# Float64 weights made into float32: the lower word as a rounded integer and one integer add on GpSimd

## The chip, the core and the metric

The kernel runs on one core of a Trainium2 chip. Time is device microseconds from the start to the end of one execution. Five engines run their own instruction streams: TensorE (PE, matrix products; PEld is its loading of weights), VectorE (DVE), ScalarE (ACT), GpSimd (POOL) and SyncE (SP, which here issues all DMAs). They wait for each other by semaphores.

## What is computed

Attention with pooled keys and values, and then two feed-forward layers over 4608 tokens, 512 features and 2048 hidden units:

```python
k_p, v_p = mean of k, v over 8 neighbours along the sequence
x = softmax(q @ k_p.T / sqrt(64)) @ v_p          # 8 batches, 8 heads, 576 tokens, head size 64
h = x @ moe_w_in;  g = maximum(0.01 * h, h);  x = g @ moe_w_out
h = x @ moe2_w_in
g = where(h >= 1, h, where(h <= -1, 0, (h + 1) ** 2 / 4))
out = (g @ moe2_w_out).astype(float32)
```

The four weight matrices (512x2048 and 2048x512) come in as float64. The kernel takes them in as pairs of 32-bit words and makes float32 values of the bits.

## The kernel before

Tokens are worked on in blocks of 512. Each float32 matrix is held as a high and a low part, of which three products are summed, so that every product of 128x128 by 512 columns costs three matmuls (lines 598 to 600 for the first matrix of a layer, "h", and 625 to 627 for the second, "acc").

The program is written in program order by hand: generators yield after each group of instructions, and `run` and `pump` go round them, so the text order of the yields sets what stands next to what on each engine. There are nine blocks. The first visit is block 0 with the hidden units 0 to 1023 (f = 0 to 7), the second block 1 with all 2048 (f = 0 to 15), the third block 0 again with f = 8 to 15, and then the other blocks one after another. Each visit has two slots for one f. In the first visit and before it, the attention of blocks 0 and 1 is computed beside the first weights; the weights of the first layer arrive one tile of 128x512 at a time (26 whole tiles and 12 half tiles, of 6 tiles more), until the end of the second visit. In later visits the second layer's weights are converted in halves of 128x256 (64 of them) and stored to DRAM as float32.

One weight tile is converted by `to_f32` out of `bits`, in which the low and the high word of each float64 alternate (`lo`, `hi`: each a strided view, with a step of two words). Names in the rows: `wb` is the tile of bits, `wc` the result, whose left half is `a` (the float32 value) and whose right half is `e` (the exponent), `w0i` and `w0o` the high and low parts of layer 0's two matrices. Line 108 (ScalarE) takes the absolute value of the high word read as float32, line 109 (VectorE) clamps it, line 111 (ScalarE) turns the low word into a float scaled by 2^-52, line 112 (VectorE) shifts the exponent into place, line 116 (VectorE) joins sign, exponent and the upper 20 bits of the fraction into `a`, line 120 (VectorE) masks out the power of two of `a`, line 122 (GpSimd) multiplies it with the scaled low word, and line 123 (GpSimd) adds the product to `a`. Then line 133 (ScalarE) copies `a` rounded to the high part, and line 135 (VectorE) takes the difference for the low part. Line 135 is also that of other splits (`gl`, `aL`, `aX`); in the first visit the split of `gl` is on GpSimd.

GpSimd's other work in the first visits is the normalisation of the attention weights (line 455), which follows VectorE's sums (lines 444 to 452).

Of the kernel before, what the change touches and what calls it, by code (L numbers as in the profile page):

```python
# [8 lines left out]
F32 = mybir.dt.float32  # L9
F32R = mybir.dt.float32r  # L10
U32 = mybir.dt.uint32
AF = mybir.ActivationFunctionType
ALU = mybir.AluOpType
# [22 lines left out]
def attention_moe_moe2(ctx: ExitStack, tc: tile.TileContext, qT, kT, v, k01, v01, w_in1, w_out1, w_in2, w_out2, out):  # L36
# [5 lines left out]
    nc = tc.nc  # L42
# [40 lines left out]
    def bits_load(key, part, n, tile_of):  # L83

        layer, kind, f = key
        t = tile_of([P, 2 * DM // n], U32, f"wb{layer}{kind}{f}_{part}")
        w_in, w_out = w_bits[layer]
        if kind == "i":
            kn = KT // n
            src = w_in[part * kn * P:(part + 1) * kn * P, 2 * f * P:2 * (f + 1) * P]  # L90
            nc.sync.dma_start(
                out=t.rearrange("p (k c) -> p k c", k=kn), in_=src.rearrange("(k p) c -> p k c", p=P)
            )
        else:
            nc.sync.dma_start(out=t, in_=w_out[f * P:(f + 1) * P, 2 * DM // n * part:2 * DM // n * (part + 1)])
        w_raw[key, part] = t

    def to_f32(key, part, n, tile_of):


        layer, kind, f = key
        bits = w_raw.pop((key, part)).rearrange("p (n t) -> p t n", t=2)
        lo, hi = bits[:, 0], bits[:, 1]
        c = tile_of([P, 2 * DM // n], U32, f"wc{layer}{kind}{f}_{part}")
        a, e = c[:, 0:DM // n], c[:, DM // n:]
        ef, lof = e.bitcast(F32), lo.bitcast(F32)
        w_f32[key, part] = a.bitcast(F32)
        nc.scalar.activation(out=ef, in_=hi.bitcast(F32), func=AF.Abs)
        nc.vector.tensor_scalar(out=ef, in0=ef, scalar1=LEAST, scalar2=MOST, op0=ALU.max, op1=ALU.min)
        yield True  # L110
        nc.scalar.activation(out=lof, in_=lo, func=AF.Copy, scale=2.0**-52)
        nc.vector.tensor_scalar(
            out=e, in0=e, scalar1=5, scalar2=2, op0=ALU.logical_shift_left, op1=ALU.logical_shift_right
        )
        yield True
        nc.vector.scalar_tensor_tensor(
            out=a, in0=hi, scalar=0xC0000000, in1=e, op0=ALU.bitwise_and, op1=ALU.bitwise_or
        )
        yield True
        nc.vector.tensor_scalar(out=e, in0=a, scalar1=0xFF800000, scalar2=None, op0=ALU.bitwise_and)  # L120
        yield True
        nc.gpsimd.tensor_tensor(out=ef, in0=lof, in1=ef, op=ALU.mult)
        nc.gpsimd.tensor_tensor(out=a.bitcast(F32), in0=a.bitcast(F32), in1=ef, op=ALU.add)

    def w_tiles(key):
        layer, kind, f = key
# [11 lines left out]
    def f32_keep(key, part, n):  # L138
        hi, lo = w_tiles(key)
        return split(hi[:, cols(part, n)], lo[:, cols(part, n)], w_f32.pop((key, part)))  # L140
# [1025 lines left out]
    with tc.manual_schedule():  # L1166
# [3 lines left out]
            out=mask, in_=ident[0:96, 0:96].rearrange("p (g c i) -> p c g i", g=3, c=4), axis=AX.XY, op=ALU.add  # L1170
# [28 lines left out]
        def first_weights(key, part, n, raw_of, f32_of):  # L1199

            bits_load(key, part, n, raw_of)
            yield True
            yield True
            turn = to_f32(key, part, n, f32_of)
            for step in (1, 3, 1, 0):
                for _ in range(step):
                    next(turn, None)
                yield True
            yield from f32_keep(key, part, n)
# [3 lines left out]
        def later_weights():  # L1213

            i = state["late"]
            state["late"] += 1
            gens = []
            if 0 <= i - 2 < len(rest_jobs):
                key, part, n, _, tile_of = rest_jobs[i - 2]
                gens.append(to_f32(key, part, n, tile_of))  # L1220
            if 0 <= i - 4 < len(rest_jobs):
                gens.append(f32_keep(*rest_jobs[i - 4][:3]))
            if i < len(rest_jobs):
                loads.append((bits_load, *rest_jobs[i][:4]))
            return gens
# [8 lines left out]
        def weights_up_to(n):  # L1234
            for job in jobs[state["step"]:n]:
                active.append(first_weights(*job))
            state["step"] = max(state["step"], min(n, len(jobs)))
# [79 lines left out]
        def second_weights(load):  # L1317
            def turn(h):
                yield from to_f32(*h, f32_tile)
                f32_store(*h)  # L1320

            gens = [turn(h) for h in pending2]
            n = state["step2"]
            state["step2"] += 1
            pending2[:] = halves2[len(halves2) * n // n_steps2:len(halves2) * (n + 1) // n_steps2] if load else []
            for h in pending2:
                loads.append((bits_load, *h, raw_tile))
            return gens
# [91 lines left out]
```

## Time and profile before

| | |
|---|---|
| median of 3 runs | 1757.46 us (1756.05 to 1760.45) |
| span of the profiled execution, first to last instruction | 1755.2 us |
| TensorE busy | 1674.8 us, 95% of the span |
| VectorE busy | 1204.4 us, 69% |
| ScalarE busy | 868.3 us, 49% |
| GpSimd busy | 662.7 us, 38% |
[...]

The profiled execution has no time of its own beside its span, so the span is held against the median of the runs; the two differ by 2.3 us, which covers what lies around the first and the last instruction and the difference from run to run. Busy shares are means over stages: to see what one stage waits for, it is read by itself, with the busy time of each engine in it and with the chain of work that ended last. [...] "Idle before" is time in which an engine had nothing running, and what ended it.

### The profile page before, as it was taken

Reading aid. Unit: us, or ns where it says so; the run is one execution under the profiler, and the core shown is the slowest. Engines: PE = TensorE matmul, PEld = TensorE weight load, DVE = VectorE, ACT = ScalarE, POOL = GpSimd, SP = SyncE. Lnnn points to the kernel's source line nnn. Section 1 sums busy time; section 2 is a strip of 40 time slices with the busy share of each in tenths; the row PEclk is TensorE's granted clock in tenths of the full one; section 3 lists DMA queues with packets and bytes.
Section 4 is the critical chain, followed back from the end, with each engine's and each line's share of the span. In section 5 each row is a group of like instructions: output and inputs, shape, how many; then the busy total and the mean of one; then the engine's idle time right before and its main releaser. Section 6 shows DMA issues by size and latency. Waiting matters only on the chain.

```text
span 1755.2 us, 27818 instructions
## 1 busy us (share of the span) xinstructions
PE 1674.8 (95%) x9372; PEld 1477.4 (84%) x9372; DVE 1204.4 (69%) x2294; ACT 868.3 (49%) x1873; POOL 662.7 (38%) x750
## 2 busy tenths in 40 slices
PE   6778999999999999999999999999999799999998
PEld 4566778778888888888888898899899799999998
DVE  7987864565655555564435577877866788887967
ACT  4545443434444343443334566776666444544444
POOL 4664521222222222221224345454443525242525
PEclk9889999999999999999999999999999999999999
DMA  6423332323232231322222264564435873444231
GB/s 211 138 83 96 121 123 78 99 68 112 69 102 82 69 109 55 115 75 72 58 94 57 77 227 170 182 237 168 172 135 206 313 253 123 137 150 140 103 109 61
DMA packets 154223, 221.51 MB, mean 126 GB/s; under 512 B 18592, under 2 KB 95392, under 8 KB 154080
## 3 DMA queue, kind: packets, MB, share of 16 engines
q1 hardware_dynamic: 154080, 219.73, 38.6%
q8 instruction: 74, 1.21, 0.3%
q14 instruction: 69, 0.57, 0.1%
HBM read 136.84 MB, written 82.84 MB: 125 GB/s over the span
## 4 chain that ended last, share of the span: by engine, by line
PE 70%; DVE 15%; DMA 6%; issue 4%; ACT 3%; POOL 1%; SPq 0%; DVEq 0%; ACTq 0%; POOLq 0%
PE u L1083 20%; PE acc L625 6%; PE acc L626 6%; PE acc L627 6%; PE h L598 6%; PE h L599 6%; PE h L600 6%; PE Y L841 4%; PE V L841 2%; PE X L841 2%; PE sc L422 2%; PE tm L478 1%; DMA g<-tV 1%; DVE xs L702 1%; DVE tW L893 1%
## 5 line engine op out<-in xcount | busy, mean ns | idle before, releaser
L1083 PE MATMUL u<-v,m 128*128 128x256 f32 x3024 | 366.9, 284 | 8.0 <-DVE m L1048 8.0
L1083 PEld LDWEIGHTS u<-v,m 128*128 128x128 f32 x3024 | 364.8, 192 | 10.1 <-DVE m L1048 9.7
L1048 DVE TENSOR_TENSOR m<-m,m 128x512 fp32r<-128x512 f32 (+1 forms) x280 | 249.7, 922 | 55.2 <-ACT m L1043 47.6
L1043 ACT ACTIVATE m<-m 128x512 fp32r<-128x512 f32 (+1 forms) x280 | 162.8, 588 | 190.8 <-PE u L1083 134.5
L626 PE MATMUL acc<-gl,w0o 128*128 128x512 f32 x576 | 228.2, 396 | 10.2 <-DVE gl L135 10.2
L625 PE MATMUL acc<-gh,w0o 128*128 128x512 f32 x576 | 233.0, 405 | 1.3 <-ACT gh L133 1.2
L599 PE MATMUL h<-xl,w0i 128*128 128x512 f32 x576 | 226.6, 393 | 6.4 <-DVE xl L184 5.6
L598 PE MATMUL h<-xh,w0i 128*128 128x512 f32 x576 | 230.4, 400 | 0.3 <-DMA xh<-xk 0.3
L135 DVE TENSOR_TENSOR gl<-t,gh 128x512 fp32r<-128x512 f32 x136 | 102.0, 750 | 185.5 <-ACT gh L133 179.9
L627 PE MATMUL acc<-gh,w0o 128*128 128x512 f32 x576 | 226.8, 394 | 0.0
L600 PE MATMUL h<-xh,w0i 128*128 128x512 f32 x576 | 226.2, 393 | 0.0
L609 ACT ACTIVATE t<-h 128x512 f32<-128x512 f32 x144 | 85.9, 597 | 188.3 <-PE h L600 110.3
L455 POOL TENSOR_TENSOR at<-at,r 128x32 f32<-128x32 f32 (+3 forms) x160 | 75.3, 491 | 198.7 <-DVE r L452 185.9
L626 PEld LDWEIGHTS acc<-gl,w0o 128*128 128x128 f32 x576 | 109.4, 190 | 34.0 <-DVE gl L135 13.5
L599 PEld LDWEIGHTS h<-xl,w0i 128*128 128x128 f32 x576 | 109.1, 189 | 29.6 <-DVE xl L184 6.7
L625 PEld LDWEIGHTS acc<-gh,w0o 128*128 128x128 f32 x576 | 109.2, 190 | 27.1 <-ACT gh L133 3.1
L598 PEld LDWEIGHTS h<-xh,w0i 128*128 128x128 f32 x576 | 109.3, 190 | 23.9 <-DMA xh<-xk 1.1
L627 PEld LDWEIGHTS acc<-gh,w0o 128*128 128x128 f32 x576 | 109.3, 190 | 23.3
L600 PEld LDWEIGHTS h<-xh,w0i 128*128 128x128 f32 x576 | 109.0, 189 | 22.9
L882 POOL TENSOR_SCALAR tV<-tV 128x384 f32<-128x384 f32 x48 | 58.4, 1216 | 151.4 <-ACT tV L874 126.0
L841 PE MATMUL Y<-xs,v 128*128 128x384 f32 x432 | 87.1, 338 | 8.7 <-DVE p L860 8.1
L133 ACT ACTIVATE gh<-t 128x512 fp32r<-128x512 f32 x144 | 91.0, 632 | 4.5
(280 smaller groups left out, 3199.9 us busy)
## 6 DMA issues: line engine op xcount, KB each, us to landing
m<-g SPq DMA_DIRECT2D x128, 256.0 KB
w2d<-w2o SPq DMA_DIRECT2D x56, 256.0 KB
v<-w2d SPq DMA_DIRECT2D x28, 512.0 KB
x<-o SPq DMA_DIRECT2D x36, 256.0 KB
xr<-x SPq DMA_DIRECT2D x24, 384.0 KB
g<-tX SPq DMA_DIRECT2D x48, 192.0 KB
g<-tV SPq DMA_DIRECT2D x48, 192.0 KB
g<-tW SPq DMA_DIRECT2D x48, 192.0 KB
```

The lines of the kernel that those rows point to most:

```text
L133: nc.scalar.activation(out=hi, in_=src, func=AF.Copy)
L135: engine.tensor_tensor(out=lo, in0=src, in1=hi, op=ALU.subtract)
L598: nc.tensor.matmul(ph, wh[:, c], xh, start=k == 0, stop=False)
L599: nc.tensor.matmul(ph, wh[:, c], xl, start=False, stop=False)
L600: nc.tensor.matmul(ph, wl[:, c], xh, start=False, stop=k == KT - 1)
L625: nc.tensor.matmul(acc, wh[:, c], gh, start=st, stop=False)
L626: nc.tensor.matmul(acc, wh[:, c], gl, start=False, stop=False)
L627: nc.tensor.matmul(acc, wl[:, c], gh, start=False, stop=sp)
L841: nc.tensor.matmul(ps, w[:, c], x[k, i], start=begin and k == n == 0, stop=k == 1 and n == 2, skip_group_check=True,)
L1043: nc.scalar.activation(out=self.s[u][0], in_=self.unit_source(u), func=AF.Copy)
L1048: nc.vector.tensor_tensor(out=lo, in0=self.unit_source(u), in1=hi, op=ALU.subtract)
L1083: nc.tensor.matmul(ps, a[:, c], w, start=begin and i == 0, stop=f == self.NJ - 1 and i == 2, skip_group_check=True,)
```

## The change

The low word is no longer scaled to a small fraction and multiplied by the power of two of the value. It is scaled by 2^-29 and written as an integer, between 0 and 8, which is what the three lowest bits of the float32 fraction lack. One integer add on GpSimd adds it to the bits of `a`; a carry out of the fraction runs into the exponent, as it should. So line 120 on VectorE and line 122 on GpSimd go, and line 123 is replaced by the integer add. `to_f32` has one turn less, and the turns taken by `first_weights` are numbered to match.

```diff
-        ef, lof = e.bitcast(F32), lo.bitcast(F32)
+        ef = e.bitcast(F32)
...
-        nc.scalar.activation(out=lof, in_=lo, func=AF.Copy, scale=2.0**-52)
+        nc.scalar.activation(out=lo, in_=lo, func=AF.Copy, scale=2.0**-29)
...
         yield True
-        nc.vector.tensor_scalar(out=e, in0=a, scalar1=0xFF800000, scalar2=None, op0=ALU.bitwise_and)
-        yield True
-        nc.gpsimd.tensor_tensor(out=ef, in0=lof, in1=ef, op=ALU.mult)
-        nc.gpsimd.tensor_tensor(out=a.bitcast(F32), in0=a.bitcast(F32), in1=ef, op=ALU.add)
+        nc.gpsimd.tensor_tensor(out=a, in0=a, in1=lo, op=ALU.add)
...
-            for step in (1, 3, 1, 0):
+            for step in (1, 2, 1, 0):
```

What stands in a row on the engines shows that nothing else moves. The changed kernel's lines are three lower from line 123 on; its add is on line 120. First VectorE at the start of the second visit, before (`wc0i9` is the tile of f = 9 of the first matrix):

```order
L109 TENSOR_SCALAR wc0i9_0_1294<-wc0i9_0_1294 128x512
L112 TENSOR_SCALAR wc0i9_0_1294<-wc0i9_0_1294 128x512
L116 SCALAR_TENSOR_TENSOR wc0i9_0_1294<-wb0i9_0_1244,wc0i9_0_1294 128x512
L120 TENSOR_SCALAR wc0i9_0_1294<-wc0i9_0_1294 128x512
L135 TENSOR_TENSOR gl0_1_1_1306<-t0_1_1_1303,gh0_1_1_1305 128x512
L109 TENSOR_SCALAR wc0o8_0_1328<-wc0o8_0_1328 128x512
L112 TENSOR_SCALAR wc0o8_0_1328<-wc0o8_0_1328 128x512
L135 TENSOR_TENSOR w0i8_1327<-wc0i8_0_1258,w0i8_1327 128x512
L116 SCALAR_TENSOR_TENSOR wc0o8_0_1328<-wb0o8_0_1275,wc0o8_0_1328 128x512
L120 TENSOR_SCALAR wc0o8_0_1328<-wc0o8_0_1328 128x512
```

The same place of the changed kernel:

```order
L109 TENSOR_SCALAR wc0i9_0_1260<-wc0i9_0_1260 128x512
L112 TENSOR_SCALAR wc0i9_0_1260<-wc0i9_0_1260 128x512
L116 SCALAR_TENSOR_TENSOR wc0i9_0_1260<-wb0i9_0_1212,wc0i9_0_1260 128x512
L132 TENSOR_TENSOR gl0_1_1_1270<-t0_1_1_1267,gh0_1_1_1269 128x512
L109 TENSOR_SCALAR wc0o8_0_1292<-wc0o8_0_1292 128x512
L112 TENSOR_SCALAR wc0o8_0_1292<-wc0o8_0_1292 128x512
L132 TENSOR_TENSOR w0i8_1291<-wc0i8_0_1226,w0i8_1291 128x512
L116 SCALAR_TENSOR_TENSOR wc0o8_0_1292<-wb0o8_0_1241,wc0o8_0_1292 128x512
```

Line 120 is gone, and the order of the rest is as it was. Then GpSimd in the first visit, before (`at` is a tile of attention weights, `gl` the low part of the hidden units):

```order
L122 TENSOR_TENSOR wc0o3_0_740<-wb0o3_0_701,wc0o3_0_740 128x512
L123 TENSOR_TENSOR wc0o3_0_740<-wc0o3_0_740 128x512
L135 TENSOR_TENSOR gl0_0_2_758<-t0_0_2_745,gh0_0_2_757 128x512
L122 TENSOR_TENSOR wc0i5_0_779<-wb0i5_0_743,wc0i5_0_779 128x512
L123 TENSOR_TENSOR wc0i5_0_779<-wc0i5_0_779 128x512
L455 TENSOR_TENSOR at1_1_0_783<-at1_1_0_783,r1_1_0_808 64x256
```

and of the changed kernel:

```order
L120 TENSOR_TENSOR wc0o3_0_724<-wc0o3_0_724,wb0o3_0_687 128x512
L132 TENSOR_TENSOR gl0_0_2_741<-t0_0_2_729,gh0_0_2_740 128x512
L120 TENSOR_TENSOR wc0i5_0_761<-wc0i5_0_761,wb0i5_0_727 128x512
L452 TENSOR_TENSOR at1_1_0_765<-at1_1_0_765,r1_1_0_789 64x256
L452 TENSOR_TENSOR at1_1_0_765<-at1_1_0_765,r1_1_0_789 64x32
```

Each pair of lines 122 and 123 has become one instruction in the same place.

## Rows read from the trace of the kernel before

**Rows 1.** The head of the page: span, and instructions of the whole program.
```profile
span 1755.2 us, 27818 instructions
```

**Rows 2.** Stage table: start:end and length in us, busy us (xcount) per engine, clock, DMA.
```profile
41.00:124.00 83.00, 63.26 (x259) 46.95 (x258) 78.32 (x141) 43.29 (x89) 56.63 (x53) 0.85 0.36 111
145.00:192.00 47.00, 39.79 (x160) 31.07 (x160) 44.02 (x54) 22.46 (x40) 26.88 (x19) 0.93 0.47 147
192.00:245.00 53.00, 48.32 (x221) 37.99 (x220) 42.60 (x108) 28.43 (x77) 24.20 (x37) 1.00 0.28 85
400.00:960.00 560.00, 559.63 (x2628) 461.56 (x2627) 304.45 (x738) 232.32 (x538) 146.09 (x244) 1.00 0.27 83
```

**Rows 3.** Chain of work that ended last, in time order: start us, length us, what.
```profile
10.01 10.14 DMA wb0i<-in_moe_w_in_dram
...
144.02 4.54 DMA x<-o
...
168.81 1.30 issue
170.12 1.75 DVE w0o L135
```

**Rows 4.** Timeline of VectorE from 158 us on: start us, length us, engine, line, instruction.
```profile
158.64 0.42 DVE L109 TENSOR_SCALAR wc0o<-wc0o 128x512 f32<-128x512 f32 x1
159.09 1.42 DVE L112 TENSOR_SCALAR wc0o<-wc0o 128x512 uint32<-128x512 uint32 x1
160.43 1.78 DVE L135 TENSOR_TENSOR w0o<-wc0o,w0o 128x512 fp32r<-128x512 f32 x1
```

**Rows 5.** Timeline of GpSimd in the same stretch.
```profile
158.85 1.37 POOL L122 TENSOR_TENSOR wc0i<-wb0i,wc0i 128x512 f32<-128x512 f32 x1 [2.08 <-ACT wc0o L108]
160.30 1.35 POOL L123 TENSOR_TENSOR wc0i<-wc0i 128x512 f32<-128x512 f32 x1
```

**Rows 6.** Stage table of line 120 alone: VectorE's busy us (xcount), clock, DMA.
```profile
41.00:124.00 83.00, 5.55 (x13) 0.85 0.36 111
145.00:192.00 47.00, 3.84 (x9) 0.93 0.47 147
192.00:245.00 53.00, 3.53 (x12) 1.00 0.28 85
```

**Rows 7.** Stage table of line 123 alone: GpSimd's busy us (xcount).
```profile
41.00:124.00 83.00, 16.75 (x13) 0.85 0.36 111
145.00:192.00 47.00, 13.28 (x10) 0.93 0.47 147
```

**Rows 8.** Stage table of line 109 alone: VectorE's busy us (xcount).
```profile
41.00:124.00 83.00, 9.04 (x13) 0.85 0.36 111
145.00:192.00 47.00, 9.33 (x10) 0.93 0.47 147
```

**Rows 9.** Stage table of line 112 alone: VectorE's busy us (xcount).
```profile
41.00:124.00 83.00, 9.17 (x13) 0.85 0.36 111
145.00:192.00 47.00, 12.99 (x10) 0.93 0.47 147
```

**Rows 10.** Stage table of line 135 alone: busy us (xcount) of VectorE, of GpSimd.
```profile
41.00:124.00 83.00, 16.83 (x17) 8.88 (x6) 0.85 0.36 111
145.00:192.00 47.00, 13.90 (x15) 0.00 (x0) 0.93 0.47 147
```

**Rows 11.** Stage table of line 448 alone: VectorE's busy us (xcount).
```profile
41.00:124.00 83.00, 8.16 (x10) 0.85 0.36 111
```

**Rows 12.** Timeline of VectorE: lines 448, 112 and 135 with nothing on GpSimd beside them.
```profile
17.59 0.16 DVE L448 SCALAR_TENSOR_TENSOR r<-r,s 128x4 f32<-128x4 f32 x1
...
151.48 0.43 DVE L112 TENSOR_SCALAR wc0o<-wc0o 128x512 uint32<-128x512 uint32 x1
151.82 0.68 DVE L135 TENSOR_TENSOR w0i<-wc0i,w0i 128x512 fp32r<-128x512 f32 x1
```

**Rows 13.** Group of ScalarE by form: line 111, out<-in xcount | busy us, mean ns.
```profile
L111 ACT ACTIVATE wb0i<-wb0i 128x512 f32<-128x512 uint32 x14 | 9.4, 670 | 0.0
```

## Prediction

> **What bounds the kernel now.** I read the stage table first, because the share of busy time over the whole span mixes stages with different limits. From 400 to 960 us TensorE is busy 559.63 of 560 us at the full granted clock [rows 2]: nothing that another engine saves there can show. Before 245 us it is not so. From 41 to 124 us VectorE is busy 78.32 of 83 us and TensorE 63.26, and from 145 to 192 us 44.02 against 39.79 of 47 [rows 2]. The chain of work that ended last says the same: it begins with the load of the second weight tile, which lands at 20.15 us, and from there to about 192 us it is mostly VectorE on the weight conversion (lines 109 to 120 and 135), with pieces called "issue" of 1.3 us between them [rows 3]. Those pieces are not launch cost. Held against the two timelines, they are VectorE instructions that have been issued and wait for GpSimd: line 112, which takes 0.43 us undisturbed, starts at 159.09 and ends at 160.51, just behind the end of line 122 on GpSimd at 160.22; the next one, line 135, which takes 0.68 undisturbed, starts at 160.43 and ends at 162.21, behind line 123, which ends at 161.65 [rows 4, 5, 12]. So in this part of the kernel a GpSimd operation costs VectorE time, and VectorE is what the end waits for. That is where the change acts, since it takes away one operation of each engine per weight tile.
>
> **The change, part by part.** The order of TensorE, ScalarE and SyncE is the same in both programs, apart from the line numbers; VectorE loses line 120, and GpSimd has one add where lines 122 and 123 stood. The wait structure is the old one with one link less: line 111 (ScalarE) and line 116 (VectorE), then the add, then the split.
>
> *Line 120 leaves VectorE.* It is 13 instructions and 5.55 us from 41 to 124, 9 and 3.84 from 145 to 192, 12 and 3.53 from 192 to 245 [rows 6]; from 20 to 41 there are two more jobs, at 5.55 / 13 = 0.43 each 0.86 us. Where VectorE is the chain this is off the path at its full price.
>
> *One GpSimd operation leaves, with the stretch that it causes on VectorE.* The stretch is worked out line by line as busy time minus count times undisturbed length. From 41 to 124: line 109 9.04 - 13 x 0.42 = 3.6; line 112 9.17 - 13 x 0.43 = 3.6; line 135 16.83 - 17 x 0.68 = 5.3; line 448 8.16 - 10 x 0.16 = 6.6 [rows 4, 8 to 12]. That is 19.1 us of VectorE time lost beside 56.63 us of GpSimd work [rows 2], of which line 123 is 16.75 [rows 7], or 30%: 5.7 us by share. Laid event by event over the GpSimd timeline, about 5.0 us of the stretch falls beside line 123. From 145 to 192: line 109 9.33 - 4.2 = 5.1, line 112 12.99 - 4.3 = 8.7, line 135 13.90 - 15 x 0.68 = 3.7, together 17.5; line 123 is 13.28 of 26.88 us, half: 8.7 us, or 9.6 event by event. What is late next where the stretch goes is the add that stays: it comes right behind line 116, as line 122 came behind line 120, in front of the same VectorE instructions, so I leave line 122's own stretch as it is.
>
> [...]
>
> *The price of the integer add.* No row of this trace shows GpSimd adding integers. The nearest rows are the two that it replaces, 1.37 us with the low word as a strided operand and 1.35 without [rows 5]. I take 1.37, because the new add reads the same low word in the same stride. From below I bound it by nothing under 1.3 (the same two reads and one write remain), from above by the two together, 2.72.
>
> [...] No run shown here has the operation.
>
> *ScalarE writes integers.* Line 111 already reads integers and takes 0.67 us [rows 13]; an integer result is not shown. I take it as free: ScalarE is busy 43.29 of 83 us and 22.46 of 47 [rows 2], so that even twice the price, 0.67 us more in a job, lies beside other work. If that cover were gone it would be 13 x 0.67 = 8.7 us in the first stretch.
>
> *Rounding at 2^-29 in place of the product, and one turn less in the generator.* No instruction is moved past another queue's by these, as the orders show; nothing.
>
> **The sum.** From 20 to 41: 0.86, and 0.5 of stretch as an estimate (two jobs at the first stretch's 5.0 / 13 would be 0.8), 1.4. From 41 to 124 VectorE gets 5.55 + 5.0 to 5.7 = 10.6 to 11.3 us back; the chain leaves VectorE for a few us there (the first transposes and the second block's), so I take 10. From 145 to 192 it gets 3.8 + 8.7 = 12.5, but TensorE has less to give: it is idle 47 - 39.79 = 7.2, and its clock of 0.93 means 14% of the stretch at 1.2 GHz, where half is lost: 3.3. The ceiling is 10.5; the stretch opens with a store that is not shortened (the chain has a DMA of 4.54 us at 144 [rows 3]), so I take 7.5. From 192 to 245 VectorE gets 3.53 and some stretch, TensorE is idle 53 - 48.32 = 4.7: 2. After 245: 0, for TensorE is full there and the 64 half tiles of the second layer lie beside it. Together 1.4 + 10 + 7.5 + 2 = 20.9; I round down to 20, since each stage is coupled to the next by loads. The profiled execution's span is 1755.2 us [rows 1], 2.3 below the median of the runs, 1757.46, and what lies around it doesn't change; 1757.5 - 20 = 1737.5 us.
>
> **The rivals.**
> (a) *Dear add.* The integer form takes a slower path of GpSimd, up to the 2.72 us of the pair. [...] Against it: line 122, a product, and line 123, a sum, cost the same on GpSimd, so the arithmetic doesn't set the price.
> (b) *Slower than before.* The add costs more than the pair and line 120 together, 2.72 + 0.43 = 3.15 us; from there on each job holds VectorE longer than it did. At 4 us it is 0.85 x 24 jobs (2 + 13 + 9) = 20 us more, 1777 us. It would show as one GpSimd group of 512 columns above 3.1 us.
> (c) *The attention chain takes over.* From 41 to 124 TensorE runs at 0.85 of its clock, and the scores, exponentials and transposes pass from engine to engine in turn. If that order is the limit as soon as VectorE has room, the 10 us shrink to nothing, and 1.4 + 7.5 + 2 = 11 us stay: 1746.5. For it: VectorE's and TensorE's idle shares there do not add up to a free engine. Against it: VectorE is idle 4.7 of 83 us.
> (d) *Whole length given back.* If each line 123 that is gone frees VectorE for its entire 1.3 us and not only for the part during which something was held, the first stretch could give 5.55 + 16.75 = 22.3 us, capped by TensorE's idle 83 - 63.26 = 19.7; with the second at its ceiling, 1.4 + 19.7 + 10.5 + 2 = 33.6, some 1724. Against it: the rows count only 5.0 to 5.7 us of stretch beside line 123 in the first stretch, where much of VectorE's work runs beside GpSimd at its usual length. [...]
> (e) *The change has no effect where it counts*, for instance if ScalarE's integer result is so dear that it ends later than line 116: 1757.
>
> **How the numbers follow.** Forecast 0.63, (a) 0.12, (b) 0.05, (c) 0.13, (d) 0.05, (e) 0.02. About 0.3% of this time, 5.3 us, is what a measurement can tell from no change. Faster by more than that: 0.63 + 0.05 + 0.12 of (c) + 0.07 of (a) = 0.87. Within it: 0.05 of (a), 0.01 of (c), 0.02 of (e) = 0.08. Slower: 0.05. The range reaches from the sum with all its upper bounds, 1.4 + 11.3 + 10.5 + 4.7 = 28, 1729 us, over (c) to the middle of (a) at a gain of 5.5, 1752 us; (b), (d), (e) and the small end of (a), 0.17 in all, are left out.
>
> **What would show it.** In the profile after: a GpSimd add of about 1.37 us for 512 columns and 0.75 for 256; no line 120 group on VectorE; the mean of line 135's weight splits and of line 112 lower before 192 us, while line 109's or 448's stays stretched; TensorE's busy share from 41 to 192 us above the 103 of 130 us of before; every stage from 245 us on of the same length, only earlier by some 20 us. I am wrong if the add is far from 1.4 us, if the stretch doesn't fall with GpSimd's busy time, or if the first 245 us shorten and a later stage gives it back.

## The result, and the profile of the changed kernel

The changed kernel takes 1726.11 us (median of four runs, 1725.15 to 1729.18), against 1758.95 us for the kernel before in the same comparison (1756.05 to 1761.41): a ratio of 0.9823, with a 95% interval of 0.9809 to 0.9836, or 32.8 us less. The prediction was 1737.5 us, 20 less, with a range down to 1729. So the sign and the place were right, and the size was missed. A second measurement of the same kernel, further below, gave 1731.43 us.

The head of the page and its list of busy times, changed kernel (engine, busy us, share of the span, count); they answer to [rows 1] and to the table of before:

```profile
span 1723.8 us, 27635 instructions
PE 1663.2 (96%) x9372; PEld 1475.6 (86%) x9372; DVE 1144.2 (66%) x2192; ACT 868.3 (50%) x1873; POOL 562.1 (33%) x648
```

VectorE has 60 us less work and GpSimd 101; about 26 and 52 us of that lie behind 245 us of before, beside a full TensorE. The stage table of the changed kernel tells where it counted. The stretches are those of the same work as 41:124, 124:145, 145:192, 192:245 and 245:961 of before (columns as in [rows 2]):

```profile
41.00:112.00 71.00, 57.25 (x254) 42.93 (x252) 64.52 (x126) 42.07 (x88) 36.53 (x40) 0.94 0.41 129
112.00:132.00 20.00, 20.00 (x94) 16.43 (x93) 8.02 (x14) 8.76 (x16) 3.93 (x4) 1.00 0.10 33
132.00:168.00 36.00, 36.00 (x160) 29.81 (x160) 31.01 (x46) 24.38 (x45) 14.02 (x10) 1.00 0.59 192
168.00:214.00 46.00, 45.70 (x221) 38.17 (x220) 36.18 (x95) 26.85 (x74) 13.73 (x24) 1.00 0.31 94
214.00:930.00 716.00, 714.93 (x3351) 587.40 (x3351) 365.21 (x888) 293.53 (x681) 130.60 (x246) 1.00 0.28 85
```

Against [rows 2]: 83 us became 71, 47 became 36 and 53 became 46, with the same 160 and 221 matmuls in the last two. From 132 to 214 us TensorE is busy 81.7 of 82 us at the full granted clock: it waits for nobody there any more. Its waits in these two stretches (who waits, for whom, us in total, times, longest), first before, then changed:

```profile
PE acc L626 <- DVE gl L135: 10.2, 10, 2.7
PE acc L625 <- ACT gh L133: 1.2, 2, 0.9
PE av L496 <- DVE aL L135: 0.3, 1, 0.3
```
```profile
PE av L493 <- DVE aL L132: 0.3, 1, 0.3
```

Ten waits for the low part `gl`, which VectorE makes between two weight tiles, are gone. After that stage nothing more is won or given back; the row of before that answers to 214:930 has the same length, with 51 us less GpSimd work in it:

```profile
245.00:961.00 716.00, 714.48 (x3346) 586.28 (x3346) 388.75 (x950) 292.79 (x681) 181.71 (x310) 1.00 0.28 85
```

TensorE runs the same 9372 matmuls in the same order in both, so the start of the n-th can be compared. This gives each stretch's share, beside the prediction's terms. The last column is the same for the profile of the second measurement:

| of before, us | forecast | gained in the stretch, us | second measurement, us |
|---|---|---|---|
| up to 20 | 0 | -0.8 | 0.6 |
| 20 to 41 | 1.4 | 1.5 | 0.5 |
| 41 to 124 | 10 | 10.4 | 6.1 |
| 124 to 145 | 0 | 1.6 | 0.4 |
| 145 to 192 | 7.5 | 11.1 | 11.1 |
| 192 to 245 | 2 | 6.9 | 6.9 |
| after 245 | 0 | 0.5 | -0.1 |
| together | 20.9 | 31.3 | 25.5 |

(Each figure is rounded by itself.) The two profiles of one kernel differ up to 145 us and agree from there on. VectorE's own instructions, those of line 120 left aside, run ahead by 13.2 us more from 145 to 192 and by 4.7 more up to 245, 17.9 for the 18.0 of TensorE.

The new add, by form (columns as in [rows 13], then idle time before it and what ended it):

```profile
L120 POOL TENSOR_TENSOR wc1i<-wc1i,wb1i 128x256 uint32<-128x256 uint32 x32 | 23.8, 743 | 170.3 <-DVE wc1i L116 108.0 <-DVE r L449 40.1 <-issue 22.2
...
L120 POOL TENSOR_TENSOR wc0i<-wc0i,wb0i 128x512 uint32<-128x512 uint32 x14 | 19.0, 1357 | 48.2 <-DVE wc0i L116 17.7 <-ACT wb0i L111 12.2 <-ACT wc0o L108 9.0
```

1.36 us for 512 columns and 0.74 for 256, against the 1.37 that the sum took from [rows 5].

The stretch of VectorE's instructions, by the lines of [rows 8 to 11], each from the changed kernel's line windows (stretch, length, busy us with count; in the third pair the second figure is GpSimd's). Line 109:

```profile
41.00:112.00 71.00, 8.66 (x12) 0.94 0.41 129
132.00:168.00 36.00, 8.11 (x9) 1.00 0.59 192
```

Line 112:

```profile
41.00:112.00 71.00, 5.49 (x13) 0.94 0.41 129
132.00:168.00 36.00, 7.05 (x10) 1.00 0.59 192
```

Line 132, the split (135 before):

```profile
41.00:112.00 71.00, 14.57 (x17) 8.10 (x6) 0.94 0.41 129
132.00:168.00 36.00, 10.87 (x16) 0.00 (x0) 1.00 0.59 192
```

Line 445, the sum of two small tiles (448 before):

```profile
41.00:112.00 71.00, 7.57 (x10) 0.94 0.41 129
```

With the prediction's undisturbed lengths [rows 4, 12], the first stretch has 8.66 - 12 x 0.42 = 3.6 on line 109, 5.49 - 13 x 0.43 = 0 on 112, 14.57 - 17 x 0.68 = 3.0 on 132 and 7.57 - 10 x 0.16 = 6.0 on 445, together 12.6 us where it had 19.1. The second has 4.3 + 2.8 + 0 = 7.1 where it had 17.5. So 6.5 and 10.4 us are gone, for the 5.0 to 5.7 and 8.7 to 9.6 of the prediction. The shape is much as it said: line 112 is free in the first stretch and keeps 2.8 of 8.7 us in the second, where the splits are free; 109 and 445 stay held. Laid over GpSimd's timeline, line 445's long cases (0.97 to 1.24 us) all end just behind an add of line 120. Those of line 109 end behind that add in the second stretch, and in the first behind GpSimd's split of `gl` about as often. At the start of the second visit, VectorE and then GpSimd of the changed kernel (columns as in [rows 4, 5]):

```profile
139.44 0.41 DVE L109 TENSOR_SCALAR wc0i<-wc0i 128x512 f32<-128x512 f32 x1
139.89 0.43 DVE L112 TENSOR_SCALAR wc0i<-wc0i 128x512 uint32<-128x512 uint32 x1
...
142.13 1.43 DVE L112 TENSOR_SCALAR wc0o<-wc0o 128x512 uint32<-128x512 uint32 x1
143.48 0.68 DVE L132 TENSOR_TENSOR w0o<-wc0o,w0o 128x512 fp32r<-128x512 f32 x1
```
```profile
141.76 1.51 POOL L120 TENSOR_TENSOR wc0i<-wc0i,wb0i 128x512 uint32<-128x512 uint32 x1 [2.79 <-ACT wc0o L108]
```

Line 112 that meets the add ends 0.29 us behind it. The next split is free, where in [rows 4, 5] a second GpSimd operation held it for 1.78 us.

### The profile page after: what moved, and what is told of

It reads as the page before. It is cut to its first block, busy times and chain, and to the rows that moved or that the text cites. A ratio compares the mean times of both kernels' runs of the same rounds, so it can differ in the third digit from the quotient of the medians.

```text
span 1723.8 us, 27635 instructions
## 1 busy us (share of the span) xinstructions
PE 1663.2 (96%) x9372; PEld 1475.6 (86%) x9372; DVE 1144.2 (66%) x2192; ACT 868.3 (50%) x1873; POOL 562.1 (33%) x648
## 4 chain that ended last, share of the span: by engine, by line
PE 77%; DVE 10%; DMA 5%; issue 3%; ACT 2%; POOL 1%; SPq 0%; DVEq 0%; POOLq 0%; ACTq 0%
PE u L1080 21%; PE acc L622 7%; PE acc L623 7%; PE acc L624 7%; PE h L595 7%; PE h L596 7%; PE h L597 7%; PE Y L838 4%; PE X L838 2%; PE V L838 2%; PE sc L419 2%; PE tm L475 1%; DMA g<-tV 1%; DVE xs L699 1%; DMA w2d<-w2o 1%
## 5 line engine op out<-in xcount | busy, mean ns | idle before, releaser
L132 DVE TENSOR_TENSOR gl<-t,gh 128x512 fp32r<-128x512 f32 x136 | 98.0, 720 | 227.1 <-ACT gh L130 221.2
L597 PEld LDWEIGHTS h<-xh,w0i 128*128 128x128 f32 x576 | 108.4, 188 | 22.7
L452 POOL TENSOR_TENSOR at<-at,r 128x32 f32<-128x32 f32 (+3 forms) x160 | 68.8, 450 | 136.7 <-DVE r L449 119.3
```

The source lines that it names most:

```text
L132: engine.tensor_tensor(out=lo, in0=src, in1=hi, op=ALU.subtract)
L597: nc.tensor.matmul(ph, wl[:, c], xh, start=False, stop=k == KT - 1)
```

## The experiments

My theory (A in the expectations): VectorE sets the pace until 245 us, and gains from two things that add up, its own line 120 and the hold that one GpSimd operation puts on it. The rivals: one of the two is the whole of it, or it is a different thing that the change does.

**The mask alone taken away.** The kernel before without line 120; both GpSimd operations stay:

```diff
-        nc.vector.tensor_scalar(out=e, in0=a, scalar1=0xFF800000, scalar2=None, op0=ALU.bitwise_and)
```

> The kernel before without line 120: VectorE's mask is left out, so the product on GpSimd takes the shifted exponent with the upper fraction bits in it in place of the power of two (that part of the computation is changed); both GpSimd operations stay. Theory A (every microsecond of VectorE freed before 245 us comes off the time, TensorE yields all that is asked of it): 0.9 + 5.6 + 3.8 + 3.5 us of line 120 leave VectorE, some 13 us, so about 1745 us, ratio 0.9925. Rival B (what counts is how soon a converted weight is ready, and VectorE's time does not): 0.43 of the 1.8 us by which a weight comes sooner, so about 7 us, 1751. Rival C (the first half of the gain already takes up what TensorE has to give): 18 us or more, 1740.

Measured: 1744.14 us against 1756.51, ratio 0.9921 (0.9903 to 0.9938), 12.4 us less. Its rows for the stretches that answer to 41:124 and 145:192 of before:

```profile
41.00:120.00 79.00, 63.26 (x255) 47.68 (x255) 70.19 (x128) 43.14 (x89) 57.60 (x53) 0.85 0.38 117
141.00:185.00 44.00, 39.67 (x164) 31.51 (x164) 42.53 (x46) 22.65 (x40) 27.43 (x21) 0.96 0.50 157
```

The stretches answer to those of before within a microsecond or two. GpSimd's 57.60 and 27.43 us are close to the 56.63 and 26.88 of [rows 2]. VectorE's stretch over all its instructions, each against the tenth percentile of its kind in six of the kernels, is 46.7 us up to 245 of before, from 20 on, where it was 48.1. So this is line 120's price almost alone. It has 0.86 + 5.55 + 3.84 + 3.53 = 13.8 us up to 245 [rows 6], and 12.4 of them reach the end (11.6 by the starts of matmuls in the profile).

**The mask kept, one GpSimd operation less.** The changed kernel, with a mask on VectorE whose result nobody reads, in its old place:

```diff
+        nc.vector.tensor_scalar(out=e, in0=a, scalar1=0xFF800000, scalar2=None, op0=ALU.bitwise_and)
+        yield True
         nc.gpsimd.tensor_tensor(out=a, in0=a, in1=lo, op=ALU.add)
...
-            for step in (1, 2, 1, 0):
+            for step in (1, 3, 1, 0):
```

> The changed kernel with line 120's mask kept on VectorE, its result unused: the integer add on GpSimd stands for the pair, VectorE has as many instructions as before. Theory A: the stretch beside line 123 goes, 0.5 + 5 + 9.6 + 0.9 = 16 us, and a few us that GpSimd's shorter queue gives, so 1739 to 1743 us; together with the run without the mask it adds up to the whole gain of 32 us within 3 us. Rival B: about 25 us, 1733. Rival C: the two partial gains add up to clearly more than the whole.

Measured: 1736.89 us, ratio 0.9884 (0.9869 to 0.9898), 19.6 us less. The same two stretches:

```profile
41.00:118.00 77.00, 61.87 (x258) 46.16 (x257) 71.40 (x143) 43.09 (x89) 38.02 (x41) 0.88 0.38 120
138.00:177.00 39.00, 37.49 (x164) 30.42 (x163) 36.30 (x57) 23.00 (x42) 13.87 (x11) 1.00 0.56 178
```

VectorE runs as many instructions as before, but in the second stretch, with 13.87 us of GpSimd work beside it for 26.88, its busy time falls from 44.02 to 36.30 us. The stretch counted in the same way is 28.7 us, so 19.4 less, and 19.6 reach the end. The time lies 2 us below theory A's range and 4 above rival B's 1733. 12.4 + 19.6 = 32.0, beside a whole gain of 32.8 or, by the second measurement, 25.7: neither part is the whole of it, but the times alone show the sum only within the 5 us by which one kernel's measurements differ. The stretch from 145 to 245 shows it better. There the matmul starts gain 6.5 us without the mask and 11.6 with the mask kept, together 18.1, and 18.0 in both profiles of the changed kernel.

**A float add in place of the integer add.** The low word is still written as a float scaled by 2^-52 and added as a float, which leaves out the product with the power of two (that part of the computation is changed):

```diff
-        nc.scalar.activation(out=lo, in_=lo, func=AF.Copy, scale=2.0**-29)
+        lof = lo.bitcast(F32)
+        nc.scalar.activation(out=lof, in_=lo, func=AF.Copy, scale=2.0**-52)
...
-        nc.gpsimd.tensor_tensor(out=a, in0=a, in1=lo, op=ALU.add)
+        nc.gpsimd.tensor_tensor(out=a.bitcast(F32), in0=a.bitcast(F32), in1=lof, op=ALU.add)
```

> The changed kernel with the low word scaled by 2^-52 to a float and added as a float (the low word is not multiplied by the power of two, which changes that part of the computation): integer write on ScalarE and integer add on GpSimd become float, the instruction counts stay. If integers are priced as floats: the same time as the changed kernel, 1726 us within 3, and 1.34 to 1.37 us for the add of 512 columns. If the integer form is cheaper or dearer it shows in that group's mean.

Measured: 1723.1 us, ratio 0.9799 (0.9783 to 0.9816), whose interval overlaps that of the changed kernel. Its add, and line 111 writing integers (from the kernel with the mask kept):

```profile
L121 POOL TENSOR_TENSOR wc0i<-wc0i,wb0i 128x512 f32<-128x512 f32 x14 | 19.0, 1361 | 47.8 <-DVE wc0i L117 18.0 <-ACT wb0i L112 11.3 <-ACT wc0o L108 9.1
```
```profile
L111 ACT ACTIVATE wb0i<-wb0i 128x512 uint32<-128x512 uint32 x13 | 8.7, 668 | 0.0
```

1361 ns as floats, 1357 as integers; on ScalarE 668 as integers, 670 as floats [rows 13]. The integer form costs nothing; what it brings is that one operation does for three.

**The change in one place alone.** `to_f32` takes a flag for the new form, which only one of its three callers sets: `first_weights` (first visit), `later_weights` (second visit) or that of the second layer's half tiles. The core of it, the second part as in the run of the first visit:

```diff
+        if whole:
+            nc.gpsimd.tensor_tensor(out=a, in0=a, in1=lo, op=ALU.add)
+            return
...
-            turn = to_f32(key, part, n, f32_of)
+            turn = to_f32(key, part, n, f32_of, True)
```

> The change made only for the weights of the first visit and of what stands before it (16 tiles of 512 columns at most); the rest is converted as in the kernel before. Theory A: the gain that the compared traces show up to 145 us of before, 12 to 13 us, stays for good: 1745 to 1747 us. A rival by which a lead is given back later (because the second visit is bound by something that doesn't move): less than 6 us, 1753 or more.

> The change made only for the weights that are converted during the second visit (10 to 12 whole tiles and 12 half tiles); the rest as in the kernel before. Theory A: the gain of 145 to 245 us, 17 to 19 us: 1738 to 1742 us, and with the run of the first weights alone it adds up to the whole gain. By the prediction's ceiling on TensorE it would be 9.5 us, 1749.

> The change made only for the 64 half tiles of the second layer's weights, converted from 260 us on, where TensorE is full. Theory A and the prediction: no change, 1758 us within 3. If the hold on VectorE matters there as well: some us faster.

Measured: first visit alone 1748.34 us, ratio 0.995 (0.9935 to 0.9965), 8.2 less. Second visit alone 1738.72, ratio 0.9883 (0.9868 to 0.9898), 20.0 less. Second layer alone 1754.61, ratio 0.9979 (0.9968 to 0.999), 4.1 less, where none was expected. They add up to 32.3. For the second visit the stage-by-stage comparison of matmul starts has it 0.6 us behind at 145 us and 17.5 ahead at 241: the stretch from 145 on gives its 18 us by itself, without any gain ahead of it, and more than the 9.5 that the sum allowed. The first visit alone is 12.7 us ahead at 145 us and 12.5 at 231; it loses 1.6 around 253 to 262 us and 1.4 more by 454 us, and ends 9.6 ahead in that profile. No wait in the trace names the cause of these losses; I leave them open. The second layer's 4.1 us are under the 0.3% of the prediction, though the interval excludes a ratio of 1; its profile has it 1.5 us ahead by 581 us and 2.7 at the end. What gives them is open too, and theory A doesn't cover them.

**The split of `gl` moved from GpSimd to VectorE in the first visit.** If the remaining hold is still dear there, moving an operation that holds should pay for VectorE's extra work:

```diff
-        own = layer == 0 and blk == 0 and f < F0
+        own = False
```

> The changed kernel with the split of the hidden units of the first visit (8 instructions of 512 columns) on VectorE in place of GpSimd. Each costs VectorE 0.68 us of its own and takes away a GpSimd operation of 1.3 us, beside which VectorE lost about 1.0 us each before the change (6.1 us over 6). If the hold is the price: 0 to 3 us faster than the changed kernel, 1723 to 1726. If instead VectorE's own instruction count sets the stage: 8 x 0.68 = 5 us slower, 1731.

Measured: 1726.16 us against 1758.68, ratio 0.9806 (0.9789 to 0.9822), the first measurement of the changed kernel and within the spread of the second. VectorE is busy 63.81 us with 133 instructions up to about the same matmul (41 to 114 us), where the changed kernel has 64.52 with 126: what it is spared in holds, it pays in its own work. Between the two theories the time decides nothing, since they lie 5 us apart.

**The hold put back without the mask.** A second GpSimd add whose result nobody reads, behind the first; VectorE has the changed kernel's instructions. If hold is the cause, most of the second part goes again; if it was a shorter chain from line 116 to the split, nothing does:

```diff
         nc.gpsimd.tensor_tensor(out=a, in0=a, in1=lo, op=ALU.add)
+        nc.gpsimd.tensor_tensor(out=e, in0=e, in1=lo, op=ALU.add)
```

> The changed kernel with a second integer add on GpSimd right behind the live one, into the scratch half of the tile, its result unused (that add is on top of what the reference needs). The converted weight is ready as early as in the changed kernel; only GpSimd is as long busy per job as before. Theory A (a GpSimd operation holds VectorE, and VectorE's time counts): VectorE's stretch is back, some 17 to 20 us slower than the changed kernel, 1743 to 1746 us, as the kernel before without its mask (1744). Rival B (what counts is how soon the weight is ready): as the changed kernel, 1726 to 1730 us.

Measured: 1748.78 us against 1757.99, ratio 0.9947 (0.9931 to 0.9964). That is 22.7 us slower than the changed kernel's first measurement and 17.4 than its second, and some 3 us above the range of theory A. By matmul starts it gains 7.2 us from 145 to 245 of before, about what line 120's absence brings, in place of 18.0. VectorE and then GpSimd at the start of the second visit:

```profile
147.04 1.55 DVE L109 TENSOR_SCALAR wc0i<-wc0i 128x512 f32<-128x512 f32 x1
148.62 1.41 DVE L112 TENSOR_SCALAR wc0i<-wc0i 128x512 uint32<-128x512 uint32 x1
```
```profile
146.75 1.55 POOL L120 TENSOR_TENSOR wc0o<-wc0o,wb0o 128x512 uint32<-128x512 uint32 x1 [2.18 <-ACT wc0i L108]
148.25 1.50 POOL L121 TENSOR_TENSOR wc0o<-wc0o,wb0o 128x512 uint32<-128x512 uint32 x1
```

Two adds, two held instructions, each 1.0 to 1.1 us over its length of 0.42 and each ending some 0.3 behind one of the adds.

The dead add also makes GpSimd's queue longer again, and the loads of later weight tiles wait for it, since they go into the buffers that it reads: at them (lines 91 and 95) SyncE waits for GpSimd's conversion 56.8 us from 145 to 245 of before, and 36.1 from 132 to 214 of the changed kernel. In the second visit that is not the price: no engine but SyncE is recorded there as waiting for GpSimd or for a weight's load, and TensorE's waits are 6.1 us for VectorE and 1.0 for ScalarE. In the first visit it is part of it. TensorE's waits there for the attention weights that GpSimd normalises (who waits, for whom, us in total, times, longest), first before, from 41 to 124, then changed, from 41 to 112:

```profile
PE tr L461 <- POOL at L455: 4.6, 4, 2.1
```
```profile
PE tr L458 <- POOL at L452: 1.6, 1, 1.6
```

The second measurement has 2.9 us of them, the dead add 3.4. So a few microseconds of the first visit can come from GpSimd's own shorter queue and not from the hold; no run here parts the two there.

**The same time on GpSimd without reading.** Three memsets of the tile's right half instead of the dead add: much GpSimd time, and no operand read.

```diff
         nc.gpsimd.tensor_tensor(out=a, in0=a, in1=lo, op=ALU.add)
+        for _ in range(3):
+            nc.gpsimd.memset(ef, 0.0)
```

> The changed kernel with three memsets of 512 columns on GpSimd behind the live add, into the scratch half of the tile, results unused: GpSimd is busy about as long as with a dead add (by the memsets of 288 columns in the trace of before, 0.33 us each, some 0.5 us a piece), but reads nothing. If any GpSimd work of that length holds VectorE: 1740 to 1746 us. If only a GpSimd operation that reads does: 1726 to 1730 us, with VectorE's lines 112 and 135 no longer than in the changed kernel.

Measured: 1741.04 us, ratio 0.9899 (0.9884 to 0.9914), 15 us slower than the changed kernel's first measurement and 10 than its second. VectorE at the start of the second visit, then the memsets beside it (three to a row):

```profile
143.86 0.86 DVE L109 TENSOR_SCALAR wc0i<-wc0i 128x512 f32<-128x512 f32 x1
144.75 0.71 DVE L112 TENSOR_SCALAR wc0i<-wc0i 128x512 uint32<-128x512 uint32 x1
...
146.86 2.00 DVE L109 TENSOR_SCALAR wc0o<-wc0o 128x512 f32<-128x512 f32 x1 [0.20 <-ACT wc0o L108]
148.89 0.71 DVE L112 TENSOR_SCALAR wc0o<-wc0o 128x512 uint32<-128x512 uint32 x1
149.52 0.67 DVE L134 TENSOR_TENSOR w0o<-wc0o,w0o 128x512 fp32r<-128x512 f32 x1
```
```profile
143.33 1.86 POOL L122 MEMSET wc0o<- 128x512 f32 x3
...
148.05 2.01 POOL L122 MEMSET wc0i<- 128x512 f32 x3
```

Lines 109 and 112, which have one input and are of the form TENSOR_SCALAR, are held for the rest of a memset (0.86 for 0.41, 0.71 for 0.43), and at 146.86 through the add ahead of the memsets and the first of them. The split at 149.52, with two inputs, runs beside the last memset in its usual 0.67. That is a distinction which the prediction did not make. The line windows of the two kernels, in the stretch that answers to 145:192 of before: lines 109, 112 and 133 with the dead add, then lines 109, 112 and 134 with the memsets.

```profile
141.00:184.00 43.00, 10.34 (x9) 0.96 0.44 144
...
141.00:184.00 43.00, 11.60 (x9) 0.96 0.44 144
...
141.00:184.00 43.00, 14.41 (x15) 0.00 (x0) 0.96 0.44 144
```
```profile
138.00:178.00 40.00, 15.55 (x9) 0.96 0.47 148
...
138.00:178.00 40.00, 6.25 (x9) 0.96 0.47 148
...
138.00:178.00 40.00, 11.76 (x15) 0.00 (x0) 0.96 0.47 148
```

Worked out as before, VectorE is stretched by 6.6 + 7.7 + 4.2 = 18.5 us beside the dead add (the kernel before: 17.5, changed: 7.1) and by 11.8 + 2.4 + 1.6 = 15.8 beside the memsets. So beside memsets line 109, the clamp, is held most and the splits least.

The rows part the forms of VectorE's instructions: the split took 0.67 us beside a memset and 1.78 beside a sum [rows 4]; line 112 took 0.71 beside a memset and 1.42 beside a product [rows 4], for 0.43 undisturbed. Why the two forms differ no row tells.

**The small sum made a reduction.** One input alone does not keep an instruction from being held, as lines 109 and 112 show (1.55 us for 0.42 and 1.41 for 0.43 beside the dead add). But the reductions of lines 441 and 443 took their usual 0.41 and 0.17 us in the first stretch, though 15 of the 20 lie beside a GpSimd operation. Line 445, which has two inputs of four columns, is held for 6.0 us there, and may not have to be. The two partial sums go into one tile, and a reduction with one input adds them; the 1e-9 that line 445 adds is left out.

```diff
-            nc.vector.tensor_reduce(out=r2[0:n, :, 0], in_=rest, axis=AX.X, op=ALU.add)
+            nc.vector.tensor_reduce(out=r2[0:n, :, 1], in_=rest, axis=AX.X, op=ALU.add)
...
-            nc.vector.scalar_tensor_tensor(
-                out=r[0:n], in0=r[0:n], scalar=1e-9, in1=r2[0:n], op0=ALU.add, op1=ALU.add
-            )
+            nc.vector.tensor_reduce(out=r[0:n, :, 0], in_=r2[0:n], axis=AX.X, op=ALU.add)
```

> The changed kernel with the two row sums of the normalisation written side by side and added by one more reduction, in place of an addition of two tiles of 128x4 (the 1e-9, which a sum of at least 1 in float32 doesn't show, is left out). The sum of two tiles takes 0.16 us undisturbed and 0.76 on the mean from 41 to 112 us of the changed kernel (7.57 us over 10), since GpSimd holds it; reductions ran beside GpSimd at their usual length. If the hold falls on the form of VectorE's instruction: 4 to 8 us faster than the changed kernel, 1718 to 1722 us. If the wait only moves to the next VectorE instruction that is held: the same as the changed kernel, 1726 us within 2.

> As the run with the reduction, and with the first visit's 8 splits of the hidden units on VectorE. If both take a hold away: 1716 to 1722 us. If the splits' own 0.68 us each cost what their hold did, as in the run that moved them alone: the same as the run with the reduction alone.

> The changed kernel once more, beside the two runs of this call on the same chip, so that a few microseconds between them can be told: 1724 to 1728 us by every theory.

Measured side by side: the reduction 1722.94 us, ratio 0.9802 (0.9788 to 0.9817); with `gl` on VectorE as well 1722.31, ratio 0.9803 (0.979 to 0.9817); the changed kernel again 1731.43, ratio 0.9854 (0.984 to 0.9869), above the 1724 to 1728 expected of it. Line 445 with the reduction, whole first stretch:

```profile
41.00:112.00 71.00, 1.58 (x10) 0.90 0.44 136
```

0.16 us each, though eight of the ten lie beside a GpSimd operation, where it took 0.76. The reduction beats both kernels: all its runs (1718.80 to 1723.98) lie below all eight of the changed kernel (1725.15 to 1733.95), by 3.2 or 8.5 us between the medians, depending on the measurement; the 8.5 are those of the runs side by side.

The two measurements of the changed kernel differ by 5.3 us. Their profiles part mostly between 66 and 124 us, and from 145 to 245 they gain the same. TensorE from 41 to 116 us, first measurement, then second, then the kernel before:

```profile
41.00:116.00 75.00, 61.25 (x271) 45.86 (x270) 65.89 (x128) 43.23 (x90) 37.85 (x41) 0.94 0.41 130
```
```profile
41.00:116.00 75.00, 61.15 (x253) 46.02 (x252) 63.60 (x127) 42.12 (x89) 37.46 (x41) 0.86 0.40 124
```
```profile
41.00:116.00 75.00, 58.09 (x235) 43.46 (x234) 71.70 (x126) 38.30 (x79) 49.76 (x45) 0.83 0.38 117
```

The same busy time holds 271 matmuls at a granted clock of 0.94 and 253 at 0.86, and VectorE is busy no longer in the second. Of the first 260 whole microseconds of before, 215 have a granted clock of 1.00, 33 of 0.50 and the other 12 of something between; matmuls of 512 columns start 0.23 us apart at 1.00 (128.59 to 130.90 us) and 0.43 at 0.50 (124.24 to 126.80). So a mean of 0.94 is 9 of the 75 us at the half clock and the rest at the full one, 0.86 is 21 and 0.83 some 25; half of the 12 us between the first two is 6. So the 5 us go with the clock in this early stage, and of the 10.4 us gained from 41 to 124 in the first profile some 4 were a better clock than this kernel always gets: the second profile is 7.6 us ahead at 145 us, the first 12.8. Why the clock was granted differently is not shown.

## Why the prediction came out as it did

*The bound and the place.* Right. What stood before 245 us was VectorE on the weight conversion, and all but 0.5 us of the gain in the profile arose there. Later stages kept their length, as said. It holds in full from 145 us on; in the first stretch VectorE is the pace only in part, as below.

*Line 120 at its full price.* Nearly right: 13.8 us on VectorE up to 245, 12.4 at the end when taken away alone.

*The stretch beside line 123.* Right in cause, somewhat low in size: 6.5 and 10.4 us were freed for 5.0 to 5.7 and 8.7 to 9.6. From 145 us on the hold is shown as the cause by the dead add, which gave it back while no engine but SyncE waited for GpSimd. In the first stretch GpSimd's shorter queue is a second way, which the prediction did not have.

*The integer add at 1.37, ScalarE's integers free.* Right: 1.36, and 668 ns for 670. With that rivals (a), (b) and (e) fall. The gain of 5.5 us with (a), at the upper end of the range, stands in no run: the add took half of the 2.72 us of the pair, and the kernel gained 32.8.

*20 to 41: 1.4.* It brought 1.5 in the one profile and 0.5 in the other.

*41 to 124: 10.* At the upper end: 10.4 in one profile, 6.1 in the other, and 8.7 in that with the float add. VectorE was freed of 5.55 + 6.5 = 12.0 us there, so not all of it came through. That the first figure fits is in part luck with the clock. Rival (c), by which nothing of the 10 stays, falls: the first visit alone brings 12.7 us by 145.

*145 to 245: 7.5 + 2.* This is the step that failed; it brought 11.1 + 6.9 = 18.0, in the second measurement's profile too, and the error is 8.5 of the 11.3 us between forecast and profile (31.3 for the rounded 20). It has two parts. First, VectorE's freed time, 12.5 + 3.53 and some stretch, was cut down by what TensorE had to give, 7.2 + 3.3 + 4.7 = 15.2, and that ceiling was itself too low, because idle time in these rows is less than what a wait costs. The place in TensorE's timeline before shows it:

```profile
161.95 0.39 PE L625 MATMUL acc<-gh,w0o 128*128 128x512 f32 x1
163.92 0.50 PE L626 MATMUL acc<-gl,w0o 128*128 128x512 f32 x1 [1.58 <-DVE gl L135]
164.26 0.39 PE L627 MATMUL acc<-gh,w0o 128*128 128x512 f32 x1
```

Matmuls that follow one another start 0.23 us apart, though each is recorded with 0.39. Here the start came 1.97 after the last one, 1.74 late, and the next another 0.11 late, while the row counts 1.58 of idle time. The ceiling was to be had from [rows 2] without any idle time: in a stage where TensorE is full, 2628 matmuls take 560 us, 0.213 each. The 160 + 221 of these stretches need 81 us, and they had 100: 19 us to give, not 15.2. The changed kernel does them in 82. No run gives the clock in GHz, as the term of 3.3 has it; the trace of before shows 0.50 of full speed from 172 to 178 us, where matmuls start 0.43 us apart for 0.23.

Second, I went 5.7 us below the ceiling, 10.5 to 7.5 for the store at the stretch's opening and 4.7 to 2 with no reason of its own, and took another 0.9 off the whole for the coupling by loads. None of that was seen: the chain's 4.54 us DMA at 144 [rows 3] lay beside a TensorE that is busy without a gap until 149 us, and VectorE's own instructions move ahead by 13.2 us from 145 to 192 (line 109 from 144.50 to 131.26, line 116 from 191.57 to 165.13), close to the 3.84 + 10.4 that it was freed of. VectorE was the pace, and its time came through almost in full.

*124 to 145: 0.* It brought 1.6. Before, the granted clock in it was 0.92, after 1.00; 8% of 21 us is 1.7. In the second profile it brought 0.4.

*Rival (d), the whole length given back.* Its time, 1724, is near, but not its mechanism. It wanted 19.7 us between 41 and 124, which gave 10.4 or less, and its 10.5 and 2 behind 145 us were the same low terms.

The range's lower end, 1729, was built with that ceiling. The second measurement, 1731.43, lies inside it, the first, 1726.11, does not; but the second lies inside only because its first stretch brought less, and the term from 145 to 245 is off by 8.5 us in both.

## What to carry to other kernels

Where VectorE sets the pace, price a GpSimd operation by the VectorE time that it holds as well as by its own (here 10.4 us of VectorE for ten such operations from 145 to 192 us), and try whether a VectorE instruction beside it can be written as a reduction (0.76 us became 0.16 here); one input alone was not enough (line 112, 1.43 for 0.43). To find what a faster engine can bring to a TensorE that waits, multiply its matmuls by the step they have where it is full and of the same size, and take that from the stage's length; idle time in the trace was less here (15.2 us with the clock's share, where the step gives 19). If TensorE waits in a stage for the freed engine alone, take the freed time in full up to that ceiling, with no discount for couplings that no row shows. Where it waits for several engines and its clock changes, as from 41 to 124 us here, only part came through: 10.4 or 6.1 of 12.0.

## What the runs showed of the hardware

- Beside a memset of 512 columns on GpSimd, VectorE's one-input TENSOR_SCALAR of 512 columns was held (0.86 for 0.41 us) and a two-input instruction was not (0.67, memset run). Beside a two-input operation on GpSimd both were held (1.43 for 0.43, changed kernel; 1.78 for 0.68, kernel before).
- A two-input VectorE instruction of four columns was held too: 0.16 us became 0.76 on the mean of ten in the changed kernel; as a reduction over both it took 0.16.
- GpSimd's 32-bit integer add cost what its float add did, 1357 and 1361 ns for 512 columns, and an integer result cost ScalarE nothing (668 and 670 ns).
- The same kernel got a mean granted clock of 0.94 or 0.86 in the same early 75 us, and its two measurements lie 5 us apart.
